# The transposed state of a recurrence: transposed from the new state instead of updated by its own products

## The chip, the cores and the metric

The kernel runs on one core of a Trainium2 chip. The metric is the time of one execution in microseconds on the device. The engines are PE (TensorE, matrix products, results in PSUM), DVE (VectorE), ACT (ScalarE), POOL (GpSimd) and SP, whose queue issues the DMAs. Each engine works through its own list of instructions in order, and semaphores make one wait for another.

## The reference, cut to what matters

Per head (4 batches by 8 heads, so 32 heads, 768 steps, head dimension 40) a state S of 40 by 40 is carried from step to step, and after it two dense layers follow:

```python
for t in range(S):
    y[:, :, t] = np.einsum('bhd,bhde->bhe', rt, state)
    Sa = np.einsum('bhde,bhe->bhd', state, at)
    state_decay = state * wt[:, :, None, :] - np.einsum('bhd,bhe->bhde', Sa, bt)
    state = state_decay + np.einsum('bhd,bhe->bhde', vt, kt)
...
x = _moe_ref(x=x, **moe_kwargs)      # 320 -> 1024 -> 320, softmax-weighted unit and layer norm between
return _moe2_ref(x=x, **moe2_kwargs) # 320 -> 2048 -> 320, leaky unit between
```

## The kernel before, in words

The first phase works through the 768 steps in 24 chunks of 32 steps (NG = 24, numbered 0 to 23; two chunks are one window of 64). `slot(g)` writes out one chunk. Four chunks share one inversion of small triangular matrices (tiles LMN), so chunks come in groups of four: g % 4 of 0, 1, 2, 3. In a chunk the recurrence is a fixed row of stages on PE: `stage_x`, `stage_u`, `stage_uf` (twice), `stage_st` (twice), `stage_g2` (two halves), `stage_s` (twice), `stage_y`. Each stage is some dozens of small matmuls into one PSUM tile of 2 KB per partition out of a ring of four (`ps_at`), and an instruction or more of DVE or ACT that brings the result into SBUF. A ring of four means that a fifth tile waits until the first has been read.

The state is kept twice: as it stands (rows of the tile VUS, brought forward by `stage_st`) and transposed (rows of the tile KBS, brought forward by `stage_s`). `stage_st` multiplies the tokens of the chunk (line 545, tile pst) and DVE adds the old state to it (line 550); where a group ends (g % 4 == 3) POOL multiplies the new state by a factor (line 553). `stage_s` comes later in PE's list, behind both halves of `stage_g2`. It does the same for the transposed state: products of the same tokens in the other order (line 568, tile pss) and a DVE addition of the old transposed state (line 576). Only where a group ends it works otherwise: PE transposes the new state VUS through a product with the identity (line 565), and ACT copies it out (line 574). `stage_st` and `stage_s` are each called for pe = 0 and pe = 1, and each call has two additions or copies, one for either half of the partitions. So a chunk has four instructions of line 550 and four of line 576 or 574. The transposed state of chunk g is read by `stage_y` of chunk g + 1.

Around this the chunk holds the work that prepares later chunks (`prep_scan`: scans on DVE, lines 279 to 301, and range checks on ACT, line 257, in chunks with g % 4 == 0; `gen1`, lines 332 to 347; `trans`, line 469; the weights' decoding, lines 724 to 733), the inversion's 31 steps on DVE (lines 362 and 366, tiles tmp and LMN; begun by line 374 in chunks with g % 4 == 2, ended by line 395 in chunks with g % 4 == 3 and read by `stage_u`, line 510, of the next), and the first dense layer of earlier tokens (lines 643 to 716: products h, softmax and norm on DVE, ACT and POOL, transposes ptr, products po, copy xs on ACT, line 701, transposes ptx). The second phase, from about 746 us, is the second dense layer (lines 1088 to 1108).

PE's order is the order in which the program is written; `pace` and `wait` put work of the dense layer and filler matmuls between the stages by tables of numbers. The orders of DVE, ACT, POOL and SP come from a scheduler that places each instruction by its own estimates of when the inputs are there.

Of the kernel before, what the change touches and what calls it, by code (L numbers as in the profile page):

```python
# [13 lines left out]
ALU = mybir.AluOpType  # L14
# [34 lines left out]
def tile_kernel(ctx: ExitStack, tc: tile.TileContext, w_fm, a0_fm, a_fm, kb_fm, r_fm, v_fm, v_tm,  # L49
                w1_in, w1_out, g_ln, w2_in, w2_out, alpha, ident_d, mask_d, tri_d, r, k, v, w, a, b, w1_nat, out,  # L50
                manual=True):
    nc = tc.nc
# [45 lines left out]
    ident = cm.tile([128, 128], F32, name="ident")  # L98
# [11 lines left out]
    KBS = [t.rearrange("p (e s d) -> p e s d", e=2, d=D) for t in KBP]  # L110
# [6 lines left out]
    VUS = [ca.tile([128, 2, 16, 40], F32, name=f"VUS{i}") for i in range(2)]  # L117
# [77 lines left out]
    def pace(dt, n):  # L195

        note(dt, n)
        floor, extra = LEVELS[min(st["slot"] // 4, 1) if st["slot"] != 4 else 2] if st["slot"] < NG - 4 else LEVELS[3]
        if more() and counted(dt + 0.09) + n < floor:
            note(0.09, 0)  # L200
            while more() and counted() < floor + extra:
                pop()
# [7 lines left out]
    def wait(g, name):  # L210
        k = (g if g < 4 else 4 + g % 4 if g < NG - 4 else 8 + g % 4, name)
        idle(WT.get(k, 0.0))
# [341 lines left out]
                                        op=ALU.mult)  # L554

    def stage_s(g, pe):
        k, kn, v, vn = KBS[g % 3], KBS[(g + 1) % 3], VUS[g % 2], VUS[(g + 1) % 2]
        last = g % 4 == 3
        wait(g, "s%d" % pe)
        p_ = ps_at.tile([128, 8, 40], F32, name="pss", tag="at")  # L560
        for p in range(8):
            for e, o in EO:
                q, s = slice(64 * e, 64 * e + 64), pe * 8 + p
                if last:
                    nc.tensor.matmul(p_[o:o + 40, p, :], lhsT=vn[o:o + 40, e, s, :], rhs=ident[o:o + 40, o:o + 40],
                                     start=True, stop=True)
                else:
                    nc.tensor.matmul(p_[o:o + 40, p, :], lhsT=v[q, e, s, :], rhs=k[q, 1 - e, s, :], start=True, stop=True)
            pace(0.104, 74)
        for e, o in EO:  # L570
            sl = slice(pe * 8, pe * 8 + 8)
            d = kn[o:o + 40, 1 - e, sl, :]
            if last:
                nc.scalar.copy(out=d, in_=p_[o:o + 40])
            else:
                nc.vector.tensor_tensor(out=d, in0=p_[o:o + 40], in1=k[o:o + 40, 1 - e, sl, :], op=ALU.add)  # L576

    def stage_g2(g, half):
        y, vuf = YS[g % 2], VUF[g % 2]
# [332 lines left out]
    def slot(g):  # L912
# [61 lines left out]
        if not fin:  # L974
            stage_s(g, 0)
            stage_s(g, 1)
# [454 lines left out]
```

## Time and profile before

| | us |
|---|---|
| median of three runs | 1146.2 |
| lowest, highest | 1144.59, 1149.14 |
| span of the profiled execution (first to last instruction) | 1140.9 |
| median of the runs less this span | 5.3 |
| PE busy, in the span | 982.9 |
| DVE busy | 769.6 |
| ACT busy | 524.2 |
| POOL busy | 480.6 |

The page gives the profiled execution's span, and no time of its own beside it; the three timed runs have what lies before the first and behind the last instruction in them as well. Busy times are sums over the whole span, so they say little about one stage: the first phase and the second have different limits. In the names, `out<-in` is what an instruction writes and reads, and a wait `A <- B` means that A stood idle until B was done. Chunks are told apart here by the copy XP (line 500), of which each chunk has one: chunk 8 from 309.7 us, 9 from 347.9, 10 from 376.4, 11 from 401.4, 12 from 426.4.

### The profile page before, as it was taken

Reading aid. Unit: us, or ns where it says so; the run is one execution under the profiler, and the core shown is the slowest. Engines: PE = TensorE matmul, PEld = TensorE weight load, DVE = VectorE, ACT = ScalarE, POOL = GpSimd, SP = SyncE. Lnnn points to the kernel's source line nnn. Section 1 sums busy time; section 2 is a strip of 40 time slices with the busy share of each in tenths; the row PEclk is TensorE's granted clock in tenths of the full one; section 3 lists DMA queues with packets and bytes.
Section 4 is the critical chain, followed back from the end, with each engine's and each line's share of the span. In section 5 each row is a group of like instructions: output and inputs, shape, how many; then the busy total and the mean of one; then the engine's idle time right before and its main releaser. Section 6 shows DMA issues by size and latency. Waiting matters only on the chain.

```text
span 1140.9 us, 38025 instructions
## 1 busy us (share of the span) xinstructions
PE 982.9 (86%) x16456; PEld 814.8 (71%) x16456; DVE 769.6 (67%) x1527; ACT 524.2 (46%) x1202; POOL 480.6 (42%) x505
## 2 busy tenths in 40 slices
PE   7677774788878897888878887989999999999997
PEld 3445453667666776776667676788999999988897
DVE  8887898778987889688878856557433444444443
ACT  3446553565656564656455747656212121212121
POOL 6576554443444444434344325235333333333332
PEclk9789786998988988888888879999999999999999
DMA  5543434343424434433334333354202020201000
GB/s 171 134 123 99 113 113 115 97 120 104 102 85 120 121 78 107 106 109 80 101 103 116 106 85 99 107 153 161 66 1 70 1 70 1 70 1 47 1 24 15
DMA packets 104690, 99.74 MB, mean 87 GB/s; under 512 B 38084, under 2 KB 83908, under 8 KB 104516
## 3 DMA queue, kind: packets, MB, share of 16 engines
q1 hardware_dynamic: 104516, 97.24, 30.9%
q8 instruction: 131, 2.15, 0.8%
q14 instruction: 43, 0.35, 0.1%
HBM read 71.78 MB, written 25.43 MB: 85 GB/s over the span
## 4 chain that ended last, share of the span: by engine, by line
PE 51%; DVE 23%; ACT 9%; POOL 5%; issue 5%; DMA 5%; SPq 1%; POOLq 0%; DVEq 0%; ACTq 0%
PE ph L1088 15%; PE h L643 6%; PE acc L1108 5%; PE acc L1107 5%; PE acc L1106 5%; DMA kbf<-in_kb_fm_dram 2%; PE pf L533 2%; DVE KBS L576 2%; DVE VUS L550 2%; DVE tmp L362 2%; DVE LMN L366 2%; DVE H L283 1%; PE py L608 1%; PE ptr L682 1%; PE po L696 1%
## 5 line engine op out<-in xcount | busy, mean ns | idle before, releaser
L1095 POOL TENSOR_TENSOR gll<-gt,gh 128x512 fp32r<-128x512 f32 (+1 forms) x112 | 127.8, 1141 | 224.6 <-ACT gh L1094 223.5
L663 DVE TENSOR_SCALAR gt<-ph,al 128x512 f32<-128x512 f32 (+1 forms) x112 | 75.5, 674 | 188.6 <-PE ph L1088 188.4
L1094 ACT CAST gh<-gt 128x512 fp32r<-128x512 f32 (+1 forms) x112 | 62.5, 559 | 254.5 <-DVE gt L664 213.8
L643 PE MATMUL h<-w1h,xt 128*128 128x512 f32 x240 | 106.8, 494 | 18.9 <-ACT h L652 16.8
L318 POOL TENSOR_TENSOR XS<-XS,H 40x512 f32<-40x512 f32 (+1 forms) x48 | 66.8, 1396 | 94.1 <-DVE H L283 64.5
L1107 PE MATMUL acc<-w2l,gh 128*128 128x320 f32 x288 | 89.0, 309 | 0.0
L1106 PE MATMUL acc<-w2h,gh 128*128 128x320 f32 x288 | 89.0, 309 | 0.0
L1108 PE MATMUL acc<-w2h,gll 128*128 128x320 f32 x288 | 88.9, 309 | 0.0
L596 POOL TENSOR_TENSOR YS<-YS,mask 64x512 f32<-64x512 f32 x48 | 62.3, 1298 | 50.5 <-ACT YS L595 48.8
L643 PEld LDWEIGHTS h<-w1h,xt 128*128 128x128 f32 x240 | 51.3, 225 | 28.6 <-ACT h L652 18.5
L664 DVE SCALAR_TENSOR_TENSOR gt<-ph,gt 128x512 f32<-128x512 f32 (+1 forms) x112 | 68.8, 615 | 3.7
L643 PE MATMUL h<-w1l,xt 128*128 128x512 f32 x144 | 68.1, 473 | 0.0
L696 PE MATMUL po<-wo1h,lnh 128*128 128x320 f32 x192 | 66.8, 348 | 0.5 <-DVE lnl L688 0.5
L217 PE MATMUL busy<-busy 128*128 128x512 bf16 x231 | 65.5, 435 | 1.3 <-POOL lims L129 1.3
L366 DVE TENSOR_TENSOR LMN<-LMN,tmp 128x87 f32<-128x87 f32 (+8 forms) x135 | 63.3, 469 | 2.6
L698 PE MATMUL po<-wo1h,lnl 128*128 128x320 f32 x192 | 61.7, 321 | 0.9 <-DVE lnl L688 0.9
L697 PE MATMUL po<-wo1l,lnh 128*128 128x320 f32 x192 | 61.5, 320 | 0.0
L362 DVE TENSOR_TENSOR tmp<-LMN,LMN 128x87 f32<-128x87 f32 (+8 forms) x135 | 59.0, 437 | 2.6
L1088 PE MATMUL ph<-w1h,w2h 128*128 128x512 f32 x180 | 59.3, 394 | 0.0
L649 ACT ACTIVATE P<-h,sm 128x1024 f32<-128x1024 f32 x24 | 26.8, 1115 | 65.9 <-DVE sm L648 63.4
L342 DVE TENSOR_TENSOR XS<-pg,mask 32x256 f32<-32x256 f32 x96 | 39.8, 414 | 23.6 <-ACT LMN L347 20.0
L1106 PEld LDWEIGHTS acc<-w2h,gh 128*128 128x128 f32 x288 | 54.2, 188 | 1.5
(216 smaller groups left out, 2706.8 us busy)
## 6 DMA issues: line engine op xcount, KB each, us to landing
kbf<-in_kb_fm_dram SPq DMA_DIRECT2D x24, 416.0 KB
x2d<-x SPq DMA_DIRECT2D x24, 320.0 KB
xd<-Y SPq DMA_DIRECT2D x24, 256.0 KB
xt<-xd SPq DMA_DIRECT2D x12, 512.0 KB
raw<-in_w_in_dram SPq DMA_DIRECT2D x20, 256.0 KB
wt<-in_w_fm_dram SPq DMA_DIRECT2D x24, 211.7 KB
raw<-in_w_in_dram SPq DMA_DIRECT2D x8, 512.0 KB
raw<-in_w_out_dram SPq DMA_DIRECT2D x16, 256.0 KB
```

Source lines behind the costliest of these rows:

```text
L318: (nc.vector if w < 2 and e in DA else nc.gpsimd).tensor_tensor(out=o, in0=o, in1=h, op=ALU.mult)
L362: eng.tensor_tensor(out=tv[:, a - rows[0][0]:b - rows[0][0]], in0=M[:, a:b, s:s + 1].to_broadcast(sh), in1=l.unsqueeze(1).to_broadcast(sh) ...
L366: r = eng.tensor_tensor(out=o, in0=o, in1=tv[:, a - rows[0][0]:b - rows[0][0]], op=ALU.add)
L643: nc.tensor.matmul(st["h"][:, ns], lhsT=l, rhs=r, start=j == 0, stop=j == len(ops) - 1)
L663: nc.vector.tensor_scalar(out=tmp, in0=h, scalar1=0.0, scalar2=al, op0=ALU.min, op1=ALU.mult)
L664: nc.vector.scalar_tensor_tensor(out=o, in0=h, scalar=0.0, in1=tmp, op0=ALU.max, op1=ALU.add)
L696: nc.tensor.matmul(po, lhsT=lh[:, k], rhs=wo1h[:, k], start=k == 0, stop=False)
L1088: nc.tensor.matmul(p, lhsT=l, rhs=r, start=j == 0, stop=j == len(ops) - 1)
L1095: nc.gpsimd.tensor_tensor(out=gll, in0=t, in1=f32(gh), op=ALU.subtract)
L1106: nc.tensor.matmul(acc, lhsT=gh[:, cs], rhs=oh, start=f == 0, stop=False)
L1107: nc.tensor.matmul(acc, lhsT=gh[:, cs], rhs=ol, start=False, stop=False)
L1108: nc.tensor.matmul(acc, lhsT=gll[:, cs], rhs=oh, start=False, stop=f == K2 - 1)
```

## The change

`stage_s` does in every chunk what it did before only where a group ends: PE multiplies the new state VUS of the next chunk by the identity, and ACT copies the result to KBS. The products of line 568 and the DVE additions of line 576 are gone from the 18 chunks that had them (chunks 0 to 22 without 3, 7, 11, 15 and 19; chunk 23 has no `stage_s`). The number of matmuls, their order on PE, the filler and the tables stay.

```diff
--- before.py
+++ after.py
@@ -554,26 +554,16 @@
                                         op=ALU.mult)
 
     def stage_s(g, pe):
-        k, kn, v, vn = KBS[g % 3], KBS[(g + 1) % 3], VUS[g % 2], VUS[(g + 1) % 2]
-        last = g % 4 == 3
+        kn, vn = KBS[(g + 1) % 3], VUS[(g + 1) % 2]
         wait(g, "s%d" % pe)
         p_ = ps_at.tile([128, 8, 40], F32, name="pss", tag="at")
         for p in range(8):
             for e, o in EO:
-                q, s = slice(64 * e, 64 * e + 64), pe * 8 + p
-                if last:
-                    nc.tensor.matmul(p_[o:o + 40, p, :], lhsT=vn[o:o + 40, e, s, :], rhs=ident[o:o + 40, o:o + 40],
-                                     start=True, stop=True)
-                else:
-                    nc.tensor.matmul(p_[o:o + 40, p, :], lhsT=v[q, e, s, :], rhs=k[q, 1 - e, s, :], start=True, stop=True)
+                nc.tensor.matmul(p_[o:o + 40, p, :], lhsT=vn[o:o + 40, e, pe * 8 + p, :], rhs=ident[o:o + 40, o:o + 40],
+                                 start=True, stop=True)
             pace(0.104, 74)
         for e, o in EO:
-            sl = slice(pe * 8, pe * 8 + 8)
-            d = kn[o:o + 40, 1 - e, sl, :]
-            if last:
-                nc.scalar.copy(out=d, in_=p_[o:o + 40])
-            else:
-                nc.vector.tensor_tensor(out=d, in0=p_[o:o + 40], in1=k[o:o + 40, 1 - e, sl, :], op=ALU.add)
+            nc.scalar.copy(out=kn[o:o + 40, 1 - e, pe * 8:pe * 8 + 8, :], in_=p_[o:o + 40])
 
     def stage_g2(g, half):
         y, vuf = YS[g % 2], VUF[g % 2]
```

The shortened function moves the later lines up by ten, so line 688 of before is line 678 after. The order of DVE, ACT, POOL and SP is placed anew by the scheduler. The first place is DVE in chunk 10, behind the inversion's first rows: VUS are the additions of `stage_st` (line 550), KBS those of `stage_s` (line 576), and `128x87`, `128x112` the steps of the inversion. Before:

```order
L362 TENSOR_TENSOR tmp_5906<-LMN0_164,LMN1_165 128x87
L550 TENSOR_TENSOR VUS1_168<-pst_5986,VUS0_167 40x320
L366 TENSOR_TENSOR LMN0_164<-LMN0_164,tmp_5906 128x3x29
L550 TENSOR_TENSOR VUS1_168<-pst_5986,VUS0_167 40x320
L362 TENSOR_TENSOR tmp_5974<-LMN0_164,LMN1_165 128x112
L550 TENSOR_TENSOR VUS1_168<-pst_6005,VUS0_167 40x320
L366 TENSOR_TENSOR LMN0_164<-LMN0_164,tmp_5974 128x4x28
L550 TENSOR_TENSOR VUS1_168<-pst_6005,VUS0_167 40x320
L362 TENSOR_TENSOR tmp_5977<-LMN0_164,LMN1_165 128x135
L688 TENSOR_TENSOR lnl_5939<-ptr_6043,lnh_5938 128x512
L366 TENSOR_TENSOR LMN0_164<-LMN0_164,tmp_5977 128x5x27
L576 TENSOR_TENSOR KBS2_158<-pss_6112,KBS1_157 40x320
```

and after:

```order
L362 TENSOR_TENSOR tmp_5906<-LMN0_164,LMN1_165 128x87
L366 TENSOR_TENSOR LMN0_164<-LMN0_164,tmp_5906 128x3x29
L362 TENSOR_TENSOR tmp_5974<-LMN0_164,LMN1_165 128x112
L366 TENSOR_TENSOR LMN0_164<-LMN0_164,tmp_5974 128x4x28
L678 TENSOR_TENSOR lnl_5939<-ptr_5940,lnh_5938 128x512
L362 TENSOR_TENSOR tmp_5977<-LMN0_164,LMN1_165 128x135
L550 TENSOR_TENSOR VUS1_168<-pst_5986,VUS0_167 40x320
L366 TENSOR_TENSOR LMN0_164<-LMN0_164,tmp_5977 128x5x27
L550 TENSOR_TENSOR VUS1_168<-pst_5986,VUS0_167 40x320
L362 TENSOR_TENSOR tmp_5980<-LMN0_164,LMN1_165 128x156
L550 TENSOR_TENSOR VUS1_168<-pst_6005,VUS0_167 40x320
L366 TENSOR_TENSOR LMN0_164<-LMN0_164,tmp_5980 128x6x26
```

The four additions of line 550 stand two steps later in the inversion, and the four of line 576 are gone. The second place is DVE at the end of the same inversion, in chunk 11, from around the addition Yt of `stage_y` (line 612 before, 602 after) to line 395 (of before the rows of lines 391 and 395 that follow are left out). Before:

```order
L612 TENSOR_TENSOR Yt_6664<-py_6630,H_3134 104x512
L362 TENSOR_TENSOR tmp_6486<-LMN0_164,LMN1_165 128x156
L655 TENSOR_SCALAR sm_6600<-sm_6600 128x1
L366 TENSOR_TENSOR LMN0_164<-LMN0_164,tmp_6486 128x26x6
L362 TENSOR_TENSOR tmp_6548<-LMN0_164,LMN1_165 128x135
L366 TENSOR_TENSOR LMN0_164<-LMN0_164,tmp_6548 128x27x5
L362 TENSOR_TENSOR tmp_6551<-LMN0_164,LMN1_165 128x112
L366 TENSOR_TENSOR LMN0_164<-LMN0_164,tmp_6551 128x28x4
L362 TENSOR_TENSOR tmp_6554<-LMN0_164,LMN1_165 128x87
L366 TENSOR_TENSOR LMN0_164<-LMN0_164,tmp_6554 128x29x3
L391 SCALAR_TENSOR_TENSOR LMN0_164<-LMN0_164,LMN1_165 128x30 x2
L714 TENSOR_TENSOR x2_6754<-ptx_6750,x2_6754 128x2x128
```

and after:

```order
L362 TENSOR_TENSOR tmp_6551<-LMN0_164,LMN1_165 128x112
L602 TENSOR_TENSOR Yt_6664<-py_6630,H_3134 104x512
L366 TENSOR_TENSOR LMN0_164<-LMN0_164,tmp_6551 128x28x4
L645 TENSOR_SCALAR sm_6600<-sm_6600 128x1
L362 TENSOR_TENSOR tmp_6554<-LMN0_164,LMN1_165 128x87
L366 TENSOR_TENSOR LMN0_164<-LMN0_164,tmp_6554 128x29x3
L391 SCALAR_TENSOR_TENSOR LMN0_164<-LMN0_164,LMN1_165 128x30 x2
L391 SCALAR_TENSOR_TENSOR LMN0_164<-LMN0_164,LMN1_165 128x31
L395 STREAM_TRANSPOSE LMN1_165<-LMN0_164 128x32x32
```

Behind Yt stood eight instructions of lines 362 and 366, and three stand there now; the copy x of line 714 has moved behind line 395. The third place is ACT in chunk 8, behind the square of the softmax (line 652 before, 642 after): H are the range checks (line 257), P the norm (line 660 before, 650 after). Before:

```order
L652 ACTIVATE h_4836,sm_5013<-P_5012,sm_5013 128x1024
L347 ACTIVATE LMN0_164<-pg_5042 32x256
L257 ACTIVATE H_5059,flags_60<-wt_4944,lims_61 104x8x64
L660 ACTIVATE P_5012<-P_5012,sm_5013 128x1024
L257 ACTIVATE H_5059,flags_60<-wt_4944,lims_61 104x8x64
L257 ACTIVATE H_5059,flags_60<-wt_4946,lims_61 104x8x64
L726 ACTIVATE em2_4953<-em2_4953,ebias_66 128x256
L727 ACTIVATE em2_4953<-em2_4953 128x256
L257 ACTIVATE H_5059,flags_60<-wt_4946,lims_61 104x8x64
L347 ACTIVATE LMN0_164<-pg_5042 32x256
```

and after:

```order
L642 ACTIVATE h_4836,sm_5013<-P_5012,sm_5013 128x1024
L347 ACTIVATE LMN0_164<-pg_5042 32x256
L566 COPY KBS0_156<-pss_5155 40x320 x2
L347 ACTIVATE LMN0_164<-pg_5042 32x256
L566 COPY KBS0_156<-pss_5183 40x320
L257 ACTIVATE H_5059,flags_60<-wt_4944,lims_61 104x8x64
L566 COPY KBS0_156<-pss_5183 40x320
L257 ACTIVATE H_5059,flags_60<-wt_4944,lims_61 104x8x64
L257 ACTIVATE H_5059,flags_60<-wt_4946,lims_61 104x8x64
L347 ACTIVATE LMN0_164<-pg_5126 32x256
L257 ACTIVATE H_5059,flags_60<-wt_4946,lims_61 104x8x64
```

The four copies of KBS stand before the second check, and the norm P has left this place; it comes behind the copy xs now.

## Rows read from the trace of the kernel before

**Rows 1.** The page: busy time of each engine, and vector engine's tenths in 40 slices
```profile
PE 982.9 (86%) x16456; PEld 814.8 (71%) x16456; DVE 769.6 (67%) x1527; ACT 524.2 (46%) x1202; POOL 480.6 (42%) x505
...
DVE  8887898778987889688878856557433444444443
```

**Rows 2.** Windows by stage: chunks 0-3, 4-19, 20-23, last phase; stretch, length, busy by engine
```profile
41.90:186.50 144.60, 112.40 (x2791) 71.88 (x2790) 122.21 (x227) 70.70 (x165) 82.24 (x76) 0.84 0.42 117
186.50:656.90 470.40, 381.94 (x9202) 312.34 (x9202) 390.54 (x850) 277.25 (x670) 192.09 (x225) 0.87 0.39 102
656.90:746.40 89.50, 77.25 (x1822) 64.22 (x1821) 51.03 (x105) 52.38 (x122) 31.12 (x34) 0.90 0.36 101
746.40:1140.90 394.50, 383.14 (x2251) 350.27 (x2247) 171.00 (x280) 102.55 (x190) 144.58 (x128) 0.99 0.16 47
```

**Rows 3.** The chain of waits, whole run: shares of the span by line
```profile
by line: PE ph L1088 15.4%; PE h L643 5.8%; issue 5.0%; PE acc L1108 4.8%; PE acc L1107 4.8%; PE acc L1106 4.8%; DMA kbf<-in_kb_fm_dram 2.4%; PE pf L533 2.1%; DVE KBS L576 1.9%; DVE VUS L550 1.8%; DVE tmp L362 1.7%; DVE LMN L366 1.6%; DVE H
```

**Rows 4.** Groups by line: count | busy, mean ns of one | idle before, releaser
```profile
L576 DVE TENSOR_TENSOR KBS<-pss,KBS 40x320 f32<-40x320 f32 x72 | 35.1, 488 | 3.2 <-PE pss L568 1.4
...
L568 PE MATMUL pss<-KBS,VUS 64*40 64x40 f32 x1152 | 28.6, 206 | 9.4 <-ACT YS L595 4.3 <-DVE VUS L550 2.6 <-DVE sm L655 2.1
...
L565 PE MATMUL pss<-ident,VUS 40*40 40x40 f32 x320 | 9.8, 215 | 9.3 <-POOL VUS L553 4.9 <-issue 4.4
...
L574 ACT COPY KBS<-pss 40x320 f32<-40x320 f32 x20 | 8.4, 420 | 4.8 <-PE pss L565 4.6
```

**Rows 5.** Windows of chunks 8, 9, 10 and 11 (columns as in rows 2)
```profile
309.70:347.90 38.20, 27.15 (x645) 22.09 (x643) 34.40 (x71) 20.78 (x53) 16.67 (x17) 0.83 0.35 95
347.90:376.40 28.50, 23.74 (x632) 19.79 (x631) 18.29 (x41) 17.03 (x43) 11.38 (x14) 0.87 0.44 117
376.40:401.40 25.00, 20.88 (x516) 16.85 (x515) 22.01 (x52) 15.35 (x40) 9.89 (x15) 0.96 0.45 116
401.40:426.40 25.00, 23.48 (x512) 19.41 (x511) 20.33 (x48) 15.47 (x35) 9.64 (x13) 0.83 0.35 87
```

**Rows 6.** Waits of PE from 186.5 to 746.4 us: total, times, longest
```profile
PE ptx L710 <- ACT xs L701: 20.8, 10, 5.7
...
PE pu L510 <- DVE LMN L395: 11.9, 4, 3.4
```

**Rows 7.** Chain of waits from 309 to 430 us: start, us, what
```profile
331.78 0.51 DVE KBS L576
...
332.76 0.48 DVE KBS L576
333.27 0.49 DVE KBS L576
...
369.77 0.49 DVE KBS L576
...
423.21 0.69 DVE Yt L612
...
428.38 2.01 DVE LMN L395
```

**Rows 8.** Vector engine's timeline in chunk 10: start, us, instruction, idle before
```profile
385.99 0.25 DVE L366 TENSOR_TENSOR LMN<-LMN,tmp 128x87 f32<-128x87 f32 x1
...
387.49 1.11 DVE L366 TENSOR_TENSOR LMN<-LMN,tmp 128x112 f32<-128x112 f32 x1
388.63 0.48 DVE L550 TENSOR_TENSOR VUS<-pst,VUS 40x320 f32<-40x320 f32 x1
```

**Rows 9.** PE's timeline in chunk 10
```profile
386.24 1.47 PE L568 MATMUL pss<-KBS,VUS 64*40 64x40 f32 x64
```

**Rows 10.** POOL's timeline in chunk 10
```profile
387.20 2.63 POOL L596 TENSOR_TENSOR YS<-YS,mask 64x512 f32<-64x512 f32 x2 [1.10 <-ACT YS L595]
```

**Rows 11.** Vector engine's timeline in chunk 14
```profile
501.81 0.48 DVE L550 TENSOR_TENSOR VUS<-pst,VUS 40x320 f32<-40x320 f32 x1
```

**Rows 12.** PE's timeline in chunk 14
```profile
502.71 1.42 PE L568 MATMUL pss<-KBS,VUS 64*40 64x40 f32 x64
```

## The prediction

> **What bounds the kernel now.** I read the page first: DVE is at 8 or 9 tenths in nearly every slice of the first 28, and at 4 in the last ones, while over the whole span PE is the busiest engine [rows 1]. So there are two programs in one, and the windows by stage part them [rows 2]. In the last phase PE is busy for 383.14 of 394.50 us, and nothing of the change lies there. In chunks 0 to 3 DVE is busy for 122.21 of 144.60 us (85%), in chunks 4 to 19 for 390.54 of 470.40 (83%), against 81% of PE, and only in chunks 20 to 23 has it slack (51.03 of 89.50, 57%). ACT has slack everywhere (277.25 of 470.40, 59%).
>
> The chain of waits says that neither engine alone sets the pace: it goes to and fro between PE, DVE and ACT, and line 576, which the change removes, holds 1.9% of it [rows 3], that is 0.019 x 1140.9 = 21.7 us. One group of four chunks shows where [rows 5]: in chunk 8 DVE is busy for 34.40 of 38.20 us, in chunk 10 for 22.01 of 25.00, in chunk 9 only for 18.29 of 28.50, and in chunk 11 PE has 23.48 of 25.00. The reader is to see that a microsecond less on DVE is worth something in chunks 8 and 10 and little by itself in 9 and 11. The waits of PE name the same places: 11.9 us in four waits of `stage_u` for the end of the inversion (line 395), which is DVE's, and 20.8 us in ten for the copy xs, which ACT gives late [rows 6]; the chain of chunk 8 passes three times through line 576 shortly before [rows 7].
>
> **The change part by part.** Removed from DVE are 72 additions of 488 ns, 35.1 us; added to ACT are 72 copies, at 420 ns by the 20 of line 574, 30.2 us [rows 4]. On PE the count stays, and a product with the identity takes 215 ns from start to end against 206 [rows 4]; they are pipelined, so I set this to nothing, covered by the overlap of 64 matmuls that start within 1.47 us [rows 9].
>
> What of the 35.1 us lay on the path, chunk by chunk:
>
> First, the end of the inversion. Each chunk of the kind of 10 loses 4 x 0.488 = 1.95 us on DVE, and the new order uses it: the addition Yt of chunk 11 stands five inversion instructions and one copy later, so less is left behind it. Behind Yt there were 12 instructions between 423.21 + 0.69 = 423.90 and 428.38 us [rows 7], 0.37 us each; six fewer are 2.2 us. The four waits for it are 3.0 us each [rows 6], so there is room. I take 2.0 each, 8 us in all. Ends: nothing, if DVE only comes earlier to a Yt that PE has not made ready; 11.9, all of the wait.
>
> Second, chunks of the kind of 8 (4, 8, 12, 16). Three of chunk 8's four additions stand on the chain, 0.51 + 0.48 + 0.49 = 1.5 us [rows 7]. In their place ACT gets its copies, 2 x 0.42 before the first range check and one more before the second, and DVE's next scan waits for the checks; but the norm P has moved away from between them. I take 1.0 each, 4 us. Ends: 1.5 each for all that is on the chain, 6 us, and minus 1.3 each, 5 us the other way, if three ACT copies stand on the path and the norm's leaving gives nothing.
>
> Third, chunks of the kind of 9. One addition of 0.49 us is on the chain there [rows 7], and ACT has 28.50 - 17.03 = 11.5 us idle for 1.7 us of copies. I take 0.5 for four chunks, 2 us. Ends: 4 x 1.95 = 8 and minus 4 x 1.7 = 7.
>
> Fourth, chunks 0, 1 and 2 lose 3 x 1.95 = 5.9 us on a DVE that is 85% busy. Here decoding of weights fills DVE and POOL, and the order changes much; I take half, 3 us, between 0 and 5.9. Chunks 20 to 22 I set to nothing: DVE's 43% of idle time covers it.
>
> Fifth, the added wait. `stage_s` now waits for the additions of line 550, and behind it on PE stand the dense layer's products po and `stage_y`, for which DVE's Yt and POOL wait. In chunk 10 the last addition ends at 388.63 + 0.48 = 389.11 [rows 8], while pss ran from 386.24, its second half from about 386.9 [rows 9]: a wait of 2.2 us. In chunk 14 it ended at 502.29 [rows 11] and pss ran from 502.71 [rows 12]: none. The additions stand two steps later now, but only because DVE is ahead. The nearest wait that exists is that of the chunks that end a group, 9.3 us of idle time before line 565 in five chunks, 1.9 each, with POOL's product on the way [rows 4]. So an end is 0, the other 18 x 1.9 = 34. I take 1.1 for the chunks like 10 (6, 10, 14, 18) and nothing elsewhere, less what later waits for DVE take up, 3 us. The wait of 2.6 us that line 568 already had for line 550 through the ring of PSUM tiles [rows 4] shows that such stalls are small.
>
> The sum is -8 - 4 - 2 - 3 + 3 = -14 us. Against the profiled span of 1140.9 that is 1127. The median of the runs stands 5.3 above this span, for what lies around it, so I forecast 1146.2 - 14 = **1132 us**. It is two thirds of the chain's 21.7.
>
> One row speaks against the first term. In chunk 10 an inversion step of line 366 takes 1.11 us, and the one before, a shorter one, 0.25 [rows 8]; POOL's mask ran from 387.20 for 2.63 us, over the slow one [rows 10], while the addition of line 550 between them took its usual 0.48. Stretched steps thus go with POOL at work, and additions that read PSUM are spared. The Trainium skill (GPSIMD Engine Reference, 1. Specifications) says that POOL shares its SBUF interfaces with VectorE and contends with DVE instructions that have two SBUF inputs. By that rule the removed additions were free cover for DVE under POOL's masks, and inversion steps that move into their place are slowed; by the rows alone the freed 1.95 us count in full. It is the third rival below.
>
> **The rivals.** (a) The stall is handed on. DVE ends earlier, but PE is near its own pace in chunk 11 (23.48 of 25.00 [rows 5]) and the weights of later chunks arrive by DMA when they do. For it: chunk 9's DVE idles for 10 us of 28.5. Against it: the waits for line 395 are plain. Then terms one and three vanish and term five is paid: -4 - 3 + 3 = -4, 1142 us.
>
> (b) Slower: the wait of `stage_s`. PE takes its list in order, and if the additions of line 550 slip behind the scheduler's plan, each of the 18 chunks pays what the group-ending chunks pay, 1.9 us, 34 in all, less the 21.7 that leave the chain: +12, 1158 us. It decides from 1.2 us a chunk on (21.7 / 18). For it: 2.2 us in chunk 10, and the two-step slip in the order. Against it: in chunk 14 there is slack, and POOL's product, for which the group-ending chunks wait, is not there in the others.
>
> (c) Inversion steps under POOL's masks. Each chunk of the kind of 10 gives back up to 2 x 0.8 us, two steps at 1.11 less 0.25, and the first term falls from 8 to 1.6: -7.6 in all, 1139 us.
>
> **How the numbers follow.** Forecast 0.57 (its own range 1121 to 1140), (a) 0.19, (b) 0.13, (c) 0.11. About 0.5%, 5.7 us, is what a measurement of this kernel can tell from no change: 1140.5 to 1151.9 is the same. Forecast and (c) are faster, 0.57 + 0.11 = 0.68; (a) is the same, 0.19; (b) slower, 0.13. The range leaves out most of (b), and some 0.05 below 1120, where nearly all 21.7 us and more come back; it reaches to (a) and some way on towards (b): 1120 to 1148.
>
> **What the profile after would show.** Right: DVE busy down by 35 and ACT up by 30 us; waits of `stage_u` for line 395 from 3.0 us to about 1; waits of pss for line 550 of about 1 us in chunks like 10, none in most others; chunks of the kinds of 8 and 10 shorter by 1 to 2 us each, and the last phase of its old length. Wrong: waits of pss of 2 us in most chunks (b); the wait for line 395 as long as before, with inversion steps of about a microsecond in the place of the additions (c); or shorter waits there and longer ones at ptx and h (a). A copy of KBS that holds up `stage_y` would be a price I have not counted.

## The result, and the profile after

The changed kernel took 1132.34 us (median of four runs, 1121.57 to 1137.78) against 1145.39 (four runs, 1139.18 to 1149.14): ratio 0.9898, 95% interval 0.9858 to 0.9938. The forecast of 1132 us holds. Its reason does not, as the experiments below show: the time was not won by taking 35 us of additions off DVE. Of all executions here one, of experiment 2, was slow (1717.05 us), and ratios leave it out.

In the changed kernel's numbering line 562 are the transposes, 566 the copies of KBS, 691 xs, 700 ptx and 678 lnl. The page of its profile, busy times by engine (answers to [rows 1]):

```profile
PE 982.7 (87%) x16456; PEld 815.6 (72%) x16456; DVE 740.3 (65%) x1455; ACT 551.9 (49%) x1274; POOL 481.6 (43%) x505
```

DVE has 29.3 us less, ACT 27.7 more. The 72 additions were 35.1, so other instructions of DVE took 5.8 us longer than before. The windows by stage (columns and stages as in [rows 2]):

```profile
44.90:189.20 144.30, 111.42 (x2786) 70.77 (x2783) 115.86 (x215) 75.01 (x176) 78.94 (x70) 0.84 0.40 113
189.20:655.70 466.50, 382.06 (x9202) 316.00 (x9202) 377.54 (x805) 297.21 (x718) 196.32 (x226) 0.87 0.40 103
655.70:740.00 84.30, 75.46 (x1823) 62.83 (x1823) 42.76 (x90) 56.66 (x134) 31.02 (x34) 0.94 0.40 110
740.00:1132.80 392.80, 381.28 (x2247) 348.40 (x2245) 169.18 (x280) 101.69 (x190) 144.57 (x128) 0.99 0.16 47
```

This execution is 8.1 us shorter than the profiled one of before: chunk 0 starts 3.0 later, chunks 0 to 3 give 0.3, chunks 4 to 19 only 3.9, chunks 20 to 23 5.2 and the last phase 1.7. The first stage had been forecast to give 3 us and the third nothing. The windows of chunks 8 to 11 (as [rows 5]):

```profile
311.20:347.40 36.20, 26.31 (x643) 22.20 (x642) 30.94 (x58) 21.78 (x56) 17.08 (x18) 0.80 0.35 94
347.40:376.00 28.60, 23.65 (x639) 19.37 (x637) 19.42 (x42) 20.46 (x51) 12.65 (x16) 0.96 0.52 135
376.00:401.60 25.60, 23.23 (x519) 19.22 (x520) 22.14 (x51) 16.46 (x43) 8.66 (x12) 0.87 0.33 88
401.60:427.30 25.70, 21.31 (x504) 17.75 (x503) 20.36 (x49) 15.19 (x35) 9.42 (x12) 0.87 0.39 89
```

Chunk 8 is 2.0 us shorter, chunks 9, 10 and 11 are 0.1 to 0.7 longer: 116.1 us for the four against 116.7. The waits of PE from 189.2 to 740 us say why so little is left (total, times, longest, as [rows 6]):

```profile
PE ptx L700 <- ACT xs L691: 24.4, 8, 6.2
PE h L633 <- ACT h L642: 11.0, 1, 11.0
PE pu L510 <- ACT XP L500: 7.9, 3, 3.6
...
PE po L686 <- DVE lnl L678: 6.7, 5, 2.5
PE pss L562 <- DVE VUS L550: 5.4, 7, 1.4
...
PE pu L510 <- DVE LMN L395: 2.6, 3, 0.9
```

The wait for the end of the inversion fell from 11.9 us to 2.6, as forecast, and that of h for the softmax's square from 16.8 to 11.0. But others are longer: for xs 24.4 us against 20.8, for XP 7.9 against 4.2, for lnl 6.7 against 0.9, and for line 550, the added one, 5.4 against 2.6. The groups by line (as [rows 4]) show the copies at their forecast price, 420 ns, and the transposes at 217:

```profile
L562 PE MATMUL pss<-ident,VUS 40*40 40x40 f32 x1472 | 43.8, 217 | 24.1 <-DVE VUS L550 7.7 <-issue 7.3 <-POOL VUS L553 5.5
L566 ACT COPY KBS<-pss 40x320 f32<-40x320 f32 x92 | 38.6, 420 | 17.7 <-PE pss L562 16.3
```

The prediction made no use of one view: the waits of SP, whose queue issues the DMAs (whole span). Line 485 loads the tokens of the next chunk but one into VUS, line 486 into YS. First the kernel before, then the changed one:

```profile
SPq L486 <- PE py L608: 64.5, 18, 8.2
...
SPq L485 <- PE pss L568: 37.3, 11, 7.8
```

```profile
SPq L486 <- PE py L598: 122.2, 17, 11.8
...
SPq L485 <- PE pst L545: 19.7, 12, 3.1
```

Before, the load into VUS waited for the products of `stage_s`, because they read the same buffer's old tokens; now it waits only for those of `stage_st`, which come earlier. SP's waits in all hardly fall by it, from 402 to 387 us in chunks 4 to 23: the load into YS, whose old tokens `stage_y` reads (line 608, then 598), now waits 122.2 us in place of 64.5. What moves is the load into VUS and what stands between the two. In SP's timeline of chunk 9 the two loads of VUS start 21.8 us after the chunk's start (at 347.90) in the kernel before, where they stand behind the weights' loads, and 10.5 us after it (at 347.38) in the changed one, where they stand ahead of one:

```profile
369.73 1.94 SPq L485 DMA_DIRECT2D VUS<-in_v_tm_dram  x2
```

```profile
357.91 0.78 SPq L485 DMA_DIRECT2D VUS<-in_v_tm_dram  x2
```

### The profile page after: what moved, and what is told of

Read it like the earlier page. It is cut to its first block, busy times and chain, and to the rows that moved or that the text cites. A ratio compares the mean times of both kernels' runs of the same rounds, so it can differ in the third digit from the quotient of the medians.

```text
span 1132.8 us, 38016 instructions
## 1 busy us (share of the span) xinstructions
PE 982.7 (87%) x16456; PEld 815.6 (72%) x16456; DVE 740.3 (65%) x1455; ACT 551.9 (49%) x1274; POOL 481.6 (43%) x505
## 4 chain that ended last, share of the span: by engine, by line
PE 50%; DVE 23%; ACT 9%; issue 7%; POOL 5%; DMA 5%; SPq 0%; DVEq 0%; POOLq 0%; ACTq 0%
PE ph L1078 15%; PE acc L1096 5%; PE acc L1097 5%; PE acc L1098 5%; PE h L633 4%; DMA kbf<-in_kb_fm_dram 3%; DVE LMN L366 2%; DVE tmp L362 2%; DVE VUS L550 2%; PE py L598 2%; DVE H L283 2%; PE po L686 2%; PE pf L533 2%; DVE kbf L309 1%; PE po L688 1%
## 5 line engine op out<-in xcount | busy, mean ns | idle before, releaser
L633 PE MATMUL h<-w1h,xt 128*128 128x512 f32 x240 | 99.0, 461 | 11.0 <-ACT h L642 11.0
L686 PE MATMUL po<-wo1h,lnh 128*128 128x320 f32 x192 | 70.7, 368 | 6.8 <-DVE lnl L678 6.7
L217 PE MATMUL busy<-busy 128*128 128x512 bf16 x231 | 70.2, 458 | 2.2 <-POOL lims L129 1.3
L688 PE MATMUL po<-wo1h,lnl 128*128 128x320 f32 x192 | 64.6, 336 | 0.2 <-DVE lnl L678 0.2
L562 PE MATMUL pss<-ident,VUS 40*40 40x40 f32 x1472 | 43.8, 217 | 24.1 <-DVE VUS L550 7.7
L633 PE MATMUL h<-w1l,xt 128*128 128x512 f32 x144 | 64.7, 449 | 0.0
L687 PE MATMUL po<-wo1l,lnh 128*128 128x320 f32 x192 | 64.6, 337 | 0.0
L366 DVE TENSOR_TENSOR LMN<-LMN,tmp 128x87 f32<-128x87 f32 (+8 forms) x135 | 60.8, 450 | 2.7
L362 DVE TENSOR_TENSOR tmp<-LMN,LMN 128x87 f32<-128x87 f32 (+8 forms) x135 | 59.9, 443 | 2.7
L562 PEld LDWEIGHTS pss<-ident,VUS 40*40 40x40 f32 x1472 | 37.5, 130 | 33.5 <-issue 14.4
L633 PEld LDWEIGHTS h<-w1h,xt 128*128 128x128 f32 x240 | 47.3, 207 | 18.1 <-ACT h L642 11.1
```

The costliest lines, as they stand in the source:

```text
L362: eng.tensor_tensor(out=tv[:, a - rows[0][0]:b - rows[0][0]], in0=M[:, a:b, s:s + 1].to_broadcast(sh), in1=l.unsqueeze(1).to_broadcast(sh) ...
L366: r = eng.tensor_tensor(out=o, in0=o, in1=tv[:, a - rows[0][0]:b - rows[0][0]], op=ALU.add)
L562: nc.tensor.matmul(p_[o:o + 40, p, :], lhsT=vn[o:o + 40, e, pe * 8 + p, :], rhs=ident[o:o + 40, o:o + 40], start=True, stop=True)
L633: nc.tensor.matmul(st["h"][:, ns], lhsT=l, rhs=r, start=j == 0, stop=j == len(ops) - 1)
L686: nc.tensor.matmul(po, lhsT=lh[:, k], rhs=wo1h[:, k], start=k == 0, stop=False)
L688: nc.tensor.matmul(po, lhsT=ll[:, k], rhs=wo1h[:, k], start=False, stop=k == K1 - 1)
```

## The experiments

Each was timed beside the kernel before on the same chip; ratios are to that. They are not the quotients of the two medians and lie up to 0.5% beside them (for experiment 2, 0.9856 against 0.9904), so a few tenths of a percent between two rows say nothing. Kind k means the chunks with g % 4 == k: chunk 8 is of kind 0, 9 of kind 1, 10 of kind 2. Experiments 2, 9 and 10 do not compute the reference's result, since their transposed state lacks an update or takes other tokens. All twelve:

| | what it does | median us | before | ratio, 95% interval |
|---|---|---|---|---|
| 1 | transposes, copies on DVE | 1132.84 | 1141.98 | 0.9906, 0.9872 to 0.9940 |
| 2 | transposes of the old state | 1130.99 | 1141.98 | 0.9856, 0.9817 to 0.9895 |
| 3 | change in kind 2 alone | 1133.04 | 1141.98 | 0.9898, 0.9865 to 0.9931 |
| 4 | change in kind 0 alone | 1140.39 | 1141.98 | 0.9965, 0.9939 to 0.9992 |
| 5 | work of before, order of 1 | 1149.91 | 1141.70 | 1.0049, 1.0017 to 1.0082 |
| 6 | work of 1, order of before | 1140.76 | 1141.70 | 1.0014, 0.9994 to 1.0034 |
| 7 | work of after, order of before | 1139.49 | 1141.70 | 0.9985, 0.9963 to 1.0006 |
| 8 | work of before, order of after | 1148.93 | 1141.70 | 1.0065, 1.0040 to 1.0091 |
| 9 | as 1, old tokens held | 1149.52 | 1141.11 | 1.0093, 1.0058 to 1.0128 |
| 10 | as 5, old tokens free | 1132.73 | 1141.11 | 0.9913, 0.9879 to 0.9948 |
| 11 | work of after, order of 1 | 1128.59 | 1141.11 | 0.9895, 0.9864 to 0.9926 |
| 12 | as 1, SP's order of before | 1157.64 | 1141.11 | 1.0142, 1.0110 to 1.0173 |

### Which part of the change wins the time: experiments 1 to 4

Experiment 1 leaves the copies on DVE (the group-ending chunks keep theirs on ACT):

```diff
-            nc.scalar.copy(out=kn[o:o + 40, 1 - e, pe * 8:pe * 8 + 8, :], in_=p_[o:o + 40])
+            (nc.scalar.copy if g % 4 == 3 else nc.vector.tensor_copy)(
+                out=kn[o:o + 40, 1 - e, pe * 8:pe * 8 + 8, :], in_=p_[o:o + 40])
```

> All 18 chunks transpose the new state, as in the changed kernel, but DVE makes the 72 copies, not ACT; the group-ending chunks keep theirs on ACT. My theory (the gain is DVE's relief, paid for with a small added wait): the 35 us are back on DVE and the added wait stays, so the gain is gone: 1145 to 1150 us, the kernel before plus 0 to 4. Rival (the gain comes from the products that fell away, or from another order of the work): most of it stays, 1132 to 1137. A 2% verdict can't part them, the interval of the ratio can: about 1.00 to 1.004 against 0.99.

Measured: 0.9906, the same gain as the change. A copy takes DVE as long as the addition did, so nothing is taken off it; the group by line, and from the waits of PE (194 to 745 us) the one for the end of the inversion, which is longer than before (11.9):

```profile
L566 DVE COPY KBS<-pss 40x320 f32<-40x320 f32 x72 | 35.1, 487 | 9.5 <-PE pss L562 8.0
```

```profile
PE pu L510 <- DVE LMN L395: 15.8, 4, 4.9
```

So the theory of the prediction falls: with DVE as busy as before (768.5 us against 769.6), nearly 1% is won.

Experiment 2 lets TensorE transpose the old state:

```diff
-        kn, vn = KBS[(g + 1) % 3], VUS[(g + 1) % 2]
+        kn, vn = KBS[(g + 1) % 3], VUS[(g + (g % 4 == 3)) % 2]
```

> As the changed kernel, but in the 18 chunks TensorE transposes the old state, not the new one, so that the stage need not wait for DVE's additions of this chunk (the update of the transposed state is left out there). It shows what the added wait costs. By my sum the wait is 3 us: 1132 - 3 = 1129, ratio to the kernel before 0.987. If the added wait is a large part that other gains have hidden (rival b in size, 7 waits of 5.4 us in all and 7.3 us of time named issue in front of these products in the changed kernel's trace): 1120 to 1125. If it costs nothing, since PE would wait for the same DVE a little later: 1132.

Measured: 0.9856, and 1130.99 us. The ratio is 0.0042 below the changed kernel's, 4.8 us, and the two intervals overlap. The forecast's 3 us for the added wait fits, but nothing is held here: the scheduler placed this kernel anew too, so the wait alone is not measured. Rival (b), 34 us of waiting, is out.

Experiments 3 and 4 make the change only in some chunks (`last = g % 4 in (2, 3)`, or `(0, 3)`, in the function of before).

> The change in chunks 2, 6, 10, 14, 18 and 22 alone (those where the inversion begins); elsewhere the products and DVE additions of the kernel before. My theory: the first term is here, four inversions that end 2 us earlier (8 us), less the added wait of 3 and 1 us of the chunk 2: 1146 - 6 = 1140, ratio 0.995, with waits of PE for the end of the inversion of about 0.9 us each in place of 3. Rival (the stall is handed on to the copy xs, whose wait grew from 20.8 to 24.4 us in the changed kernel): the waits for the inversion fall as much, but the time stays at 1145.

> The change in chunks 0, 4, 8, 12, 16 and 20 alone (scans and range checks). My second term gave 4 us for chunks 4 to 16 and some 1 us for chunk 0: 1141, ratio 0.996. Rival, from the changed kernel's trace, where ACT's copies of KBS stand on the chain of waits of chunk 8 ahead of the range checks: DVE's relief is handed to ACT, and nothing is won: 1145, ratio 1.00, the wait for xs longer than before in these chunks.

Measured: 0.9898 for chunks of kind 2 alone, the whole gain, and 0.9965 for kind 0. The first beats its forecast (0.995) by far, the second meets its own (0.996). The waits for the end of the inversion, forecast at 0.9 us each in experiment 3, are 4.9 us in 3, and its wait for xs is 29.0; in experiment 4 that for xs is 13.6, shorter than before and not longer as its rival had it. But each of these kernels also has another order of DVE, ACT, POOL and SP: against the kernel before, 298 and 248 of DVE's 1505 instructions in the main block have moved, besides the 24 that are gone, and 294 in experiment 1. A change of a few instructions can't be weighed while the scheduler moves hundreds.

### Work and order apart: experiments 5 to 8

The four kernels hold the order. To each engine's instructions but PE's, whose order is the same in all, order-only dependences are added that make a row given beforehand (shortened; held to its own order, the kernel before is the same program, instruction for instruction):

```diff
+    def hold():
+        there = {i.name: i for i in nc.cur_bb.bb.instructions}
+        for row in ORDER:
+            names = [n for n in row if n in there]
+            for a, b in zip(names, names[1:]):
+                tc.add_manual_dep(there[b], a, NoSync, reason="hold")
...
             phase2(p2)
+    hold()
     guard()
```

> The work of the kernel before, with its products, additions and waits, but DVE, ACT, POOL and SP are held to the order that the scheduler made for the first experiment (transposes, copies on DVE), by order-only dependences; PE's order is the same in both. Theory of the order (what won the time is how the scheduler placed all the rest, 294 of DVE's 1505 instructions of the main block among it): the first experiment's gain comes without its work, 1132, ratio 0.991. Theory of the work (the transposes themselves win the time, because they read other data or hold buffers for less long): 1142, ratio 1.00.

> The other half: transposes and copies on DVE, in the order of DVE, ACT, POOL and SP of the kernel before. Theory of the order: nothing is won and the added wait is paid, 1142 to 1147, ratio 1.00 to 1.005. Theory of the work: 1132, ratio 0.991.

> The changed kernel's work (transposes, copies on ACT) in the order of the kernel before: the 72 additions are simply gone from DVE's row, and the 72 copies stand in ACT's row where the scheduler puts them among the rest, whose order is held. This is DVE's relief alone. My theory of the prediction: the relief is worth 10 to 17 us without any reordering, 1127 to 1134, ratio 0.988 to 0.994. Theory of the order: 1139 to 1145, ratio 0.998 to 1.003, and most of the gain of the change lies in the order.

> The work of the kernel before in the order of the changed kernel; the 72 additions stand in DVE's row where the scheduler puts them among the rest. Theory of the order: 1130 to 1135, ratio 0.99 to 0.994. Theory of the relief: DVE has its 35 us again in an order that was made without them, so 1142 to 1148, ratio 1.00 to 1.005. Anything between would share the gain between the two.

Neither theory held: experiments 6 and 7 came out as that of the order had it, 5 and 8 against it. Order by row, work by column:

| order of | products, additions on DVE | transposes, copies on DVE | transposes, copies on ACT |
|---|---|---|---|
| before | 1 | 1.0014 | 0.9985 |
| experiment 1 | 1.0049 | 0.9906 | 0.9895 |
| after | 1.0065 | - | 0.9898 |

The transposes win nothing that can be told from noise in the old order, and the new orders lose with the old products; only the two together win. Experiment 7 is DVE's relief alone. Its page shows the 34.4 us gone from DVE (769.6 before), and its waits of PE (186 to 746 us) the one for the end of the inversion as long as before:

```profile
PE 981.6 (86%) x16433; PEld 817.1 (71%) x16456; DVE 735.2 (64%) x1455; ACT 551.2 (48%) x1274; POOL 483.3 (42%) x505
```

```profile
PE pu L511 <- DVE LMN L396: 12.3, 4, 3.4
```

(Held kernels have one line more above the code: their line 396 is 395.) With the order held, Yt still has all those instructions behind it, and a part of what DVE saves is spent waiting for Yt's input, 8.8 us more than before. DVE's waits for that, of experiment 7 and of the kernel before (186 to 746 us):

```profile
DVE Yt L603 <- PE py L599: 14.2, 8, 3.0
```

```profile
DVE Yt L612 <- PE py L608: 5.4, 6, 1.6
```

In the old order the whole of the change's work is then worth 0.0015 x 1141.7 = 1.7 us (between 4.2 gained and 0.7 lost). The copies' move from DVE to ACT is 0.9985 against 1.0014, 3.3 us; these two intervals overlap and the medians differ by 1.3 us, so it may also be nothing.

In the other direction, experiment 8 has the new order and no relief, and its wait for the end of the inversion is as short as in the changed kernel (186 to 746 us):

```profile
PE pu L511 <- DVE LMN L396: 2.7, 3, 0.9
```

What the transposes allow is seen in experiment 5, the old work in the new order. Its waits of PE (190 to 745 us), where px is the first stage of the next chunk and line 348 a copy on ACT (347 of before), and its waits of SP, where line 486 is the load into VUS:

```profile
PE px L498 <- ACT LMN L348: 20.0, 4, 6.2
```

```profile
SPq L486 <- PE pss L569: 118.4, 14, 13.2
```

In chunk 9 (from 351.40 us) the queue of SP stands still until the products are through, and the weights' load (raw, line 749) is behind it. The timeline of SP, then that of DVE:

```profile
370.85 0.78 SPq L486 DMA_DIRECT2D VUS<-in_v_tm_dram  x2
...
372.94 0.47 SPq L749 DMA_DIRECT2D raw<-in_w_out_dram  x1
```

```profile
370.26 0.99 DVE L577 TENSOR_TENSOR KBS<-pss,KBS 40x320 f32<-40x320 f32 x2 [2.47 <-PE pss L569]
...
376.11 0.29 DVE L725 TENSOR_SCALAR em<-raw 128x256 int32<-128x256 int32 x1 [4.41 <-DMA raw<-in_w_out_dram]
...
376.64 0.49 DVE L577 TENSOR_TENSOR KBS<-pss,KBS 40x320 f32<-40x320 f32 x1
```

The decoding of the weights (line 725) waits 4.41 us for its data, and the recurrence's third addition stands behind it on DVE. The chain of waits of this chunk runs the same way: products, SP's loads, the transfer of raw (3.08 us from 372.94), line 725, third addition, and on to Yt and the copy of line 348 that px waits for. So a reader of VUS holds up the state itself, by way of two queues.

### The held buffer: experiments 9, 10 and 12

That is a theory made after the fact, so it was tried from both sides. Experiment 9 is experiment 1 with the old tokens read until late, in its order:

```diff
+                q = slice(64 * e, 64 * e + 64)
+                if pe == 1 and g % 4 != 3:
+                    nc.tensor.matmul(p_[o:o + 40, p, :], lhsT=VUS[g % 2][q, e, pe * 8 + p, :], rhs=ident[q, 0:40],
+                                     start=True, stop=True)
+                else:
```

> The first experiment (transposes, copies on DVE) in its own order, but in the 18 chunks the stage's second call (pe = 1) multiplies the old tokens by the identity in place of the new state, so that half of the transposed state is wrong there, and the old tokens in VUS are read until the stage is through, as by the products of the kernel before. New theory (the release): the products read the chunk's tokens in VUS once more, late, and SP's load of the tokens of two chunks on, which goes to the same buffer, must wait for them with all that is queued behind it on SP; the transposes leave that wait out. In the fifth experiment this load waited for the products for 118.4 us in 14 waits. By it the gain is gone here: 1144 to 1150, ratio 1.002 to 1.007. Rival (something else in the transposes wins the time, such as their smaller operands or what they wait for): 1132, ratio 0.991.

Measured: 1.0093, the gain gone and more. Waits of SP, then of PE:

```profile
SPq L486 <- PE pss L565: 113.8, 15, 13.2
```

```profile
PE px L498 <- ACT LMN L348: 20.0, 4, 6.4
```

Experiment 10 is experiment 5 with the products reading another buffer:

```diff
-                    nc.tensor.matmul(p_[o:o + 40, p, :], lhsT=v[q, e, s, :], rhs=k[q, 1 - e, s, :], start=True, stop=True)
+                    nc.tensor.matmul(p_[o:o + 40, p, :], lhsT=(vn if g else v)[q, e, s, :], rhs=k[q, 1 - e, s, :], start=True, stop=True)
```

> The fifth experiment (products and additions, in the order of the first experiment) with one word changed: from chunk 1 on the products read the tokens of the next chunk and not of their own, so that the old ones are free after the state's own update (the transposed state is not the reference's). Theory of the release: the loss of the fifth experiment goes and the gain comes, 1128 to 1135, ratio 0.987 to 0.993, with products and additions as in the kernel before. Rival (the transposes are needed): as the fifth experiment, 1.005.

Measured: 0.9913. With the products and additions of before, without a transpose more, the gain is there. From chunk 1 on the load into VUS now waits for `stage_st` in place of the products (in chunk 0, which keeps its own tokens, 12.2 us for them are left), and px hardly waits (waits of SP, then of PE from 186 to 746 us):

```profile
SPq L486 <- PE pst L546: 31.0, 11, 4.4
```

```profile
PE px L498 <- ACT LMN L348: 3.4, 4, 1.0
```

Chunk 9 (from 345.62 us), SP and DVE, the same rows in the same order as in experiment 5:

```profile
355.38 0.90 SPq L486 DMA_DIRECT2D VUS<-in_v_tm_dram  x2
...
360.71 0.35 SPq L749 DMA_DIRECT2D raw<-in_w_out_dram  x1
```

```profile
361.59 0.99 DVE L577 TENSOR_TENSOR KBS<-pss,KBS 40x320 f32<-40x320 f32 x2 [0.57 <-PE pss L569]
...
363.65 1.12 DVE L725 TENSOR_SCALAR em<-raw 128x256 int32<-128x256 int32 x1
...
365.00 0.49 DVE L577 TENSOR_TENSOR KBS<-pss,KBS 40x320 f32<-40x320 f32 x1
```

From the chunk's start the load of VUS begins 19.5 us in experiment 5 and 9.8 in 10, and the third addition 25.2 and 19.4: 5.9 us, and by 5.8 us the chunk is shorter. The windows of chunk 9, experiment 5 and experiment 10 (columns as in [rows 2]):

```profile
351.40:381.00 29.60, 22.31 (x617) 18.52 (x617) 16.60 (x37) 15.49 (x38) 9.48 (x12) 0.82 0.40 105
```

```profile
345.60:369.40 23.80, 21.92 (x619) 18.27 (x620) 17.56 (x38) 15.63 (x39) 9.55 (x12) 0.86 0.46 123
```

Chunks 5, 9, 13 and 17 take 119.4 us together in experiment 5, 118.8 in 9, 107.0 in 1 and 100.3 in 10.

The changed kernel's own order shows the same places: with the old work (experiment 8) these four chunks take 128.7 us, in the changed kernel 116.4, which is 12.3 of the 18.9 us between the two profiled executions. And the decoding's waits for raw on DVE (186 to 746 us), long in experiment 8, are short in the changed kernel:

```profile
DVE em L725 <- DMA raw<-in_w_in_dram: 9.8, 4, 5.8
...
DVE em L725 <- DMA raw<-in_w_out_dram: 7.8, 4, 2.9
```

```profile
DVE em L714 <- DMA raw<-in_w_in_dram: 1.7, 3, 1.1
DVE em L714 <- DMA raw<-in_w_out_dram: 1.4, 2, 1.2
```

Experiment 12 has `hold` with SP's row of before and the others' of experiment 1:

> The first experiment with DVE, ACT and POOL in its own order, but SP's row of DMAs in the order of the kernel before, where the tokens' load stands behind the weights' loads. If the release works through SP's row (the earlier place of the loads): the gain is gone, 1140 to 1148, ratio 0.999 to 1.006. If the release only lets the transfers start earlier, whatever their row, and the order of DVE does the rest: 1132 to 1135, ratio 0.991 to 0.994.

Measured: 1.0142, worse than either theory gave. The gain goes with SP's row. That more than the gain is lost was not taken apart; a reading is that the rows of the engines must fit each other: in the waits of SP, that of the weights' write-back for POOL's decoding grows from 103.6 us in experiment 1 to 164.2 here.

```profile
SPq L775 <- POOL dec L724: 103.6, 34, 9.2
```

```profile
SPq L776 <- POOL dec L725: 164.2, 34, 17.6
```

The Trainium skill (DMA: Bandwidth & Descriptors, Issuing engines are not separate DMA queues) says that starting DMAs from several engines saves only the issue time of a sequencer, usually little. No run here moved a load to another engine. What the runs show is another thing, the order within one engine's row: with the loads all on SP, that order alone is 1.0142 against 0.9906.

### The changed kernel's work in another order: experiment 11

The changed kernel's work in the order of experiment 1 (`hold` with that row).

> The changed kernel's work (copies on ACT) in the order of the first experiment, the additions' places on DVE simply empty. In the order of the kernel before, moving the copies from DVE to ACT was worth 0.3% (0.9985 against 1.0014). If that adds to the order's gain: ratio 0.9877, 1128, below the changed kernel. If the waits of the dense layer for ACT take it up: 0.990.

Measured: 0.9895, with the lowest median of the kernels that compute all, 1128.59, but not to be told from the changed kernel's 0.9898. The relief's 0.3% can't be seen to add: from experiment 1's 0.9906 it is 0.1%, with an interval of 0.3% to either side of each.

## Why the prediction was right, and where it was wrong

The number was right by luck; the cause was not. The step that failed is the second part's heading sum, "what of the 35.1 us lay on the path, chunk by chunk": it took DVE's relief for 17 us. With the order of before held, the change's work is worth 1.7 us, from 0.7 lost to 4.2 gained (experiment 7), and with no relief at all the full gain comes (experiment 1). What stood in its place is another order together with a buffer that is free earlier, which the prediction had no term for. By the step:

- Counts and durations: right for the copies (420 ns) and ACT (+28); DVE fell by 29, not 35. Two readings are off without weight in the sum: DVE is at 8 or 9 tenths in 17 of the first 28 slices, not in nearly all, and 13 instructions stood behind Yt, not 12.
- First term, the end of the inversion, 8 us: the waits fell by 9.3 us, at about the forecast 2 us each, and that comes from the order, not the relief: experiment 7 has the relief and keeps them at 12.3, experiment 8 has the order and not the relief and they are 2.7. They didn't reach the total as 8 us: experiment 1 wins as much with 15.8 us of them, and in the changed kernel waits for xs, XP, lnl and line 550 grew. That is rival (a)'s mechanism, beside a gain that it didn't have; of its two signs the wait at ptx came, while that at h grew shorter.
- Second and third terms: chunks 4, 8, 12 and 16 are 2.9 us shorter together (155.7 to 152.8), and as `stage_u`'s waits for the inversion lie in them too, that is all that the first and second terms' 12 us left there. Chunks 5, 9, 13 and 17 are 0.5 longer, not 2 shorter. The wait for xs, which ACT copies, grew (24.4 us against 20.8); that ACT's new copies are the reason is not shown.
- Fourth term: chunks 0 to 3 gave 0.3 us, not 3; chunks 20 to 23, set to nothing, gave 5.2, most of it in chunk 20 (29.7 to 25.5 us). Experiment 8 has a chunk 20 of 26.1 us with the old work, so that comes from the order.
- Fifth term, the added wait: 3 us. The waits of pss for line 550 grew by 2.8, and experiment 6, which pays the wait in the old order, lies between 0.7 gained and 3.9 lost. It fits.
- Rival (b) is out (experiment 6). Rival (c) is out as it was priced: the inversion steps of lines 362 and 366 take 59.9 + 60.8 = 120.7 us, 122.3 before. But what it describes is there at another place, line 391 in the inversion's end, which went from 6.6 to 11.8 us (below, before and changed; also 11.8 in experiment 8, so by the order). In chunk 11 of the changed kernel one such instruction took 1.35 us and not 0.28, while POOL was at work from 426.10 for 1.30; before, the slow one there was a step of line 366, 1.25 us from 425.51, with POOL at work from 425.20 for 1.43.

```profile
L391 DVE SCALAR_TENSOR_TENSOR LMN<-LMN,LMN 128x30 f32<-128x30 f32 (+1 forms) x30 | 6.6, 258 | 3.2 <-POOL LMN L137 3.0
```

```profile
L391 DVE SCALAR_TENSOR_TENSOR LMN<-LMN,LMN 128x30 f32<-128x30 f32 (+1 forms) x30 | 11.8, 432 | 4.2 <-POOL LMN L137 3.8
```

What was missed: the products removed were counted as PE work of no cost, and the prediction didn't ask what they read. They were the last reader of the old tokens in VUS. Without them the next tokens are loaded some 10 us earlier (chunk 9), SP's queue behind that load moves, and an order of the engines becomes good that with the products loses 0.5 to 0.65%. For experiment 1 this is shown, from both sides. In the changed kernel's own order the same waits and chunks shrink, but the time is shown as a sum only: with the old work 1.0065, with the new 0.9898, with 126.1 us of waits of the VUS load for the products in the former; how much of these 1.7% is release and how much the copies on ACT was not run apart. Open is also experiment 3: it keeps the products in chunks of kinds 0 and 1 and wins the whole gain, so other orders reach it by other ways; its work and order were not taken apart.

## What to carry to other kernels

When an instruction goes, list the buffers that it read, which load waits for the last reader, and what stands behind that load in its queue; this can be worth more than the instruction's time. Busy time taken off an engine can be worth next to nothing where the row of work behind its next wait stays as long (here 34.4 us off DVE for 1.7). Where a scheduler places the work, hold its order and cross work and order before naming a cause: here a gain of 1% was in neither by itself.

## What was not expected of the hardware

One kernel's executions differ by more than most terms of the sum: 1121.57 to 1137.78 us for the changed one, so single chunks of one profile prove little. A part of this goes with TensorE's clock: the fastest of these executions had a mean granted clock of 0.913, the slowest 0.905. Within one execution, chunks 13 and 17 of the changed kernel have nearly the same work for PE, and the windows (columns as in [rows 2]) show 29.49 and 22.84 us busy for it at a mean granted clock of 0.75 and 0.93, between the two levels of 1.2 and 2.4 GHz; before either, PE worked through the chunk ahead at 0.80 and 0.81:

```profile
463.50:496.20 32.70, 29.49 (x639) 24.12 (x637) 20.53 (x42) 20.58 (x51) 12.62 (x16) 0.75 0.46 117
582.60:607.90 25.30, 22.84 (x635) 19.30 (x634) 16.51 (x36) 18.05 (x44) 10.64 (x14) 0.93 0.44 115
```

And a copy of 40 by 320 out of PSUM takes DVE 487 ns, the addition with a second operand from SBUF 488: the operand is free, and the copy no cheaper.
